# Constant matmuls and the order of all engines' work in an attention and feed-forward kernel: 70 in place of 30

## The chip, the cores and the metric

One core of a Trainium2 chip. The metric is the device time of one execution in microseconds, start to end; the figure for the kernel before is the median of 3 executions. Besides, one execution was recorded by the hardware profiler.

## What is computed

A block-sparse causal attention, and behind it a gated feed-forward layer. 4 batches, 8 heads, 768 positions, 64 values a head; 512 model columns, 1536 hidden columns; all inputs float32.

```
k_min, k_max = min, max of k over chunks of 32 positions
ub = sum_d max(q * k_min, q * k_max)          # a bound per position and chunk, causal
top_chunks = the 6 chunks with the largest ub
scores = q k^T / 8, only in those chunks and only for earlier positions
x = softmax(scores) v                          # to [3072, 512]
out = (sigmoid(x w_gate) * (x w_val)) w_out
```

## The kernel before

The 24 blocks of 128 positions are dealt out to eight units of three blocks, u0 to u7. Unit 0 takes the first block of batches 0, 1 and 2, for which no chunk has to be chosen; unit 2 takes the first block of batch 3 beside two others. A unit passes through preparing (loads, transposes, chunk minima and maxima, bounds), attention and the feed-forward layer; while TensorE does one unit's feed-forward, the next unit's attention and the preparation of the one after lie between its pieces.

Nothing of the order is decided on the chip or by a loop. The functions of the kernel only register operations with a name, the engines that may do them and what they read and write (`Plan.add`, line 48). Three long strings at the top then say everything: `ORDER` names each operation and its engine (P TensorE, A ScalarE or ACT, V VectorE or DVE, G GpSimd or POOL, S the DMA queue of SyncE), `SLOTS` gives each buffer its place, and `TIES` adds waits of one operation for another. `Plan.order` (line 77) reads them, and the kernel emits the operations in that order; every engine works its own list off from front to back, and waits where an input isn't there.

The operations that the change and the prediction speak of:

- `fl_0`, `fl_1`, ... (`keep_awake`, line 589): a constant matmul, a 128x128 block of ones times 256 columns of ones, written to a PSUM bank that nobody reads. 30 of them, all within TensorE's first 22 us.
- `kfT_b`, `qfT_b` (line 709), b = 0, 1, 2: four float32 transposes each of the first block's keys and queries; `kf16_b`, `qf16_b` (line 713) copy them out of PSUM; `scf_b` (line 748) are the scores, `expf_b_e` (line 751) the exponentials on ACT, `cmf_b_e` (line 753) the causal mask on POOL, `vc_b` (line 737) the cast of v, `pvf_b_e` (line 763), `rzf`, `xf`, `xpsf`, `xTf` (lines 766 to 779) the rest up to the transposed input of the feed-forward layer.
- `kn_u1_p`, `qn_u1_p`, `kT_u1_p`, `qT_u1_p` (`turned`, line 784), p = 0 to 3: copies and transposes of unit 1's keys and queries from the loads `k0_u1` ... `q3_u1` (line 647); `kx0`, `kx1` (line 681) their chunk minima and maxima on DVE, `kcr_u1` (line 688) the difference of these, `qf_u1_p` (line 825) and `qm_u1_p` (line 827) queries and their positive part, `kt`, `hk0`, `hk1`, `hq0`, `hq1` (lines 811 to 831) the operands of the later scores.
- `ub_u1` (line 899): 32 small matmuls for the bounds, then on DVE the choice of six chunks (`ubn`, `ubm`, `mx`, `ap`, `apt`, lines 907 to 930) and `hqm` (line 934), which carries it to the scores' operands.
- `hkp...` (line 583): eight copies of a constant pattern, 64 partitions x 1536, on any of three engines.
- `wgp`, `wg0` to `wg2`, `wv0` to `wv2`, `wo0` to `wo2` (lines 605 to 619): loads of the feed-forward weights, issued by POOL in its own list, with a cast to float16 on the way. Piece i serves the hidden blocks 4i to 4i+3, so `g_u0_8` to `g_u0_11` and `v_u0_8` to `v_u0_11` (lines 1268 and 1278: four matmuls of 384 columns each) need `wg2` and `wv2`.

All other loads are issued by SyncE, one behind the other, in the order of `ORDER`.

Of the kernel before, what the change touches and what calls it, by code (L numbers as in the profile page):

```python
# [96 lines left out]
ident=G ones16=V fl_4=P fl_2=P fl_8=P fl_3=P fl_1=P fl_0=P fl_29=P k2_u1=S kn_u1_2=A qf1_0=S kf1_0=S kf0_0=S fl_6=P fl_5=P epat0=V  # L97
ident16=V ap0=V epat=G hkp110=A hkp000=A hkp001=V kT_u1_2=P kcr0=V kt_u1_2=V hk0_u1_2=G vf1_1=G hkp011=V hkp010=G vf1_2=G hkp100=G
kf1_2=S kf0_1=S kfT_0=P kxf1=V fl_17=P fl_10=P fl_7=P kx0_u1_2=V kf16_0=V qf0_0=S qfT_0=P qf16_0=V qf1_1=S kf1_1=S kfT_1=P
kf16_1=V fl_15=P fl_16=P scf_0=P expf_0_1=A fl_19=P qf0_1=S qfT_1=P hq0=V ap1=V fl_14=P fl_9=P fl_13=P fl_11=P fl_18=P fl_12=P  # L100
qf16_1=V scf_1=P v10=G vf_0=S v16_0_0=G qf0_2=S qf1_2=S kf0_2=S expf_0_0=A cmf_0_0=G pvf_0_0=P rzf_0_0=V xf_0_0=V kx1_u1_2=V
cmf_0_1=G wgp=G kfT_2=P pvf_0_1=P qfT_2=P qf16_2=V rzf_0_1=V xf_0_1=V kxf0=V expf_1_0=A cmf_1_0=G vf_1=S vc_1=G pvf_1_0=P
rzf_1_0=V xpsf_0_0=P expf_1_1=A cmf_1_1=G pvf_1_1=P hkf0=G hk1_u1_2=A kf16_2=A scf_2=P expf_2_1=A expf_2_0=A k0_u1=S kn_u1_0=V
kT_u1_0=P xf_1_0=V fl_20=P fl_21=P wg0=G q3_u1=S qn_u1_3=A q2_u1=S rzf_1_1=V xf_1_1=V xpsf_1_1=P hq1=V xTf_1_1=V kx0_u1_0=V
kx1_u1_0=V vf_2=S wv0=G cmf_2_0=G fl_23=P xpsf_0_1=P fl_24=P fl_22=P fl_27=P xpsf_1_0=P vc_2=G xTf_1_0=V pvf_2_0=P rzf_2_0=V
xf_2_0=V q1_u1=S k3_u1=S kn_u1_3=G kT_u1_3=P hkp111=A q0_u1=S fl_28=P kx1_u1_3=V cmf_2_1=G pvf_2_1=P xpsf_2_0=P rzf_2_1=V xf_2_1=V
qT_u1_3=P qf_u1_3=V k1_u1=S qn_u1_1=A qT_u1_1=P xTf_0_0=A xTf_0_1=A qn_u1_2=A qn_u1_0=A kn_u1_1=G kT_u1_1=P kx1_u1_1=V kx0_u1_1=V
kt_u1_0=A qm_u1_3=A fl_25=P xpsf_2_1=P fl_26=P qT_u1_2=P v_0_3=S v_0_2=S v_0_1=S qf1_3=S k0_u2=S q2_u2=S k1_u2=S qf_u1_1=V
qf_u1_2=V v11=G wv1=G wg1=G hq0_u1_3=G qT_u1_0=P kt_u1_3=A hk0_u1_3=G hq1_u1_3=G wv2=G xTf_2_1=A xTf_2_0=A qf_u1_0=A qm_u1_0=A
g_u0_0=P g_u0_2=P kx0_u1_3=V kcr_f=V kcr_u1=V hkp101=V hq1_u1_0=V hkf1=V kt_u1_1=V hk0_u1_1=G wg2=G qm_u1_2=A qm_u1_1=A ub_u1=P  # L110
ubn0_u1=V ubm0_u1=V hq0_u1_1=A hq0_u1_2=A g_u0_3=P g_u0_1=P mx0_u1=V ap0_u1=V apt0_u1=V hqm0_u1_0=V v_u0_1=P v_u0_0=P v_u0_2=P
hq0_u1_0=A tanh_u0_2=A tanh_u0_1=A hg_u0_1=V ubn1_u1=V v_u0_3=P tanh_u0_3=A hg_u0_3=V ubm1_u1=V hg_u0_2=V tanh_u0_0=A hg_u0_0=V
hk0_u1_0=A hq1_u1_1=A sc_u1_0_2=P exp_u1_0_2=A sc_u1_1_2=P sc_u1_0_1=P sc_u1_0_0=P exp_u1_1_2=A sc_u1_1_0=P sc_u1_1_1=P
exp_u1_0_0=A exp_u1_0_1=A v_u0_7=P wo0=G hqm0_u1_2=G sc_u1_2_2=P exp_u1_2_2=A sc_u1_2_0=P exp_u1_2_0=A sc_u1_3_0=P sc_u1_3_2=P
exp_u1_3_2=A exp_u1_1_0=A sc_u1_3_1=P exp_u1_3_1=A exp_u1_3_0=A v16_0_3=G wo1=G v_u0_4=P sc_u1_2_1=P v_u0_6=P exp_u1_2_1=A
hk1_u1_0=G v16_0_2=G wo2=G mx1_u1=V ap1_u1=V apt1_u1=V hqm1_u1_0=V g_u0_5=P tanh_u0_5=A v_u0_5=P exp_u1_1_1=A hqm1_u1_2=A g_u0_6=P
# [285 lines left out]
def kernel(  # L402
# [192 lines left out]
    for i in range(30):  # L595
        keep_awake(i)
# [860 lines left out]
```

## Time and profile before

| | us |
|---|---|
| median of 3 executions | 281.0 (280.67 to 282.69) |
| the profiled execution | 279.88 |
| its span, first to last instruction | 278.2 |
| TensorE busy | 269.2 (97%) |
| VectorE (DVE) busy | 231.2 (83%) |
| ScalarE (ACT) busy | 180.4 (65%) |
| GpSimd (POOL) busy | 163.1 (59%) |

A row of the profile in order of time gives the start, the length, the engine, the line of the kernel, the operation, what it writes and reads, shapes, how many instructions are merged into the row, and in brackets how long the engine stood idle before and what ended that. Tile names come without their numbers: `fl<-ones` stands for all constant matmuls, `g_u` for all gate products. A row of a queue gives packets, megabytes and the share of the 16 DMA engines' time; q1 is SyncE's queue, q0 the one of POOL's weight loads. Ends of matmuls are modelled, and matmuls overlap, so that a row of several is shorter than its parts.

### The profile page before, as it was taken

The page shows a single profiled execution, that of the slowest core. Times are in us where ns is not written, and L with a number is a line of the kernel's source. Part 1 is how long each engine was busy: PE and PEld are TensorE (multiplying, and loading weights), DVE is VectorE, ACT ScalarE, POOL GpSimd, SP SyncE. Part 2 cuts the span into 40 slices and gives each one's busy share as a digit, 9 for nine tenths or more (in the row PEclk, how much of TensorE's full clock was granted, in tenths as well). Part 3 has the DMA queues.
Part 4 walks back from the last instruction along what each step waited for, and adds up shares of the span by engine and source line. Part 5 has one row for each costly group of instructions (what it writes and reads, how often), then busy time and mean ns, then how long its engine had stood idle before and what let it go on. Part 6 is the DMA issues. An engine that isn't in the chain of part 4 may idle for free.

```text
span 278.2 us, 7566 instructions
## 1 busy us (share of the span) xinstructions
PE 269.2 (97%) x2806; PEld 189.3 (68%) x2806; DVE 231.2 (83%) x686; ACT 180.4 (65%) x386; POOL 163.1 (59%) x262
## 2 busy tenths in 40 slices
PE   5979999999999999999999999999999999999995
PEld 3755658667755666557687657776888688778684
DVE  4799747687999998796999987978889998888985
ACT  6388969569858944468689979988983422341430
POOL 5797744639372873534669966724766467163440
PEclk9999999999999999999999999999999999999999
DMA  6999999999999598696896230100320033000304
GB/s 157 258 281 204 207 217 208 220 179 202 187 217 189 142 183 188 145 161 125 164 157 114 68 85 17 40 0 3 73 77 2 1 83 127 2 1 2 151 2 152
DMA packets 131717, 34.70 MB, mean 125 GB/s; under 512 B 119776, under 2 KB 128736, under 8 KB 131680
## 3 DMA queue, kind: packets, MB, share of 16 engines
q1 hardware_dynamic: 126912, 29.50, 50.6%
q0 software_dynamic: 4768, 4.72, 10.1%
q8 instruction: 22, 0.36, 0.5%
q14 instruction: 15, 0.12, 0.1%
HBM read 30.67 MB, written 6.29 MB: 133 GB/s over the span
## 4 chain that ended last, share of the span: by engine, by line
PE 87%; DMA 6%; DVE 5%; SPq 1%; issue 0%; POOL 0%; DVEq 0%
PE v_u L1259 20%; PE g_u L1259 15%; PE sc_u L957 12%; PE o_u L1308 11%; PE p_u L1082 10%; PE pv_u L990 7%; DMA wg<-in_moe_w_gate_dram 5%; PE p_g_u L1191 5%; PE ube_u L896 3%; DMA kf<-in_k_dram 1%; DVE xf L768 1%; PE kfT L709 1%; PE qfT L709 1%; PE fl L591 1%; DVE kx_u L681 1%; DVE kcr L681 1%
## 5 line engine op out<-in xcount | busy, mean ns | idle before, releaser
L968 ACT ACTIVATE att_u<-sc_u 128x512 f16<-128x512 f32 (+3 forms) x184 | 86.9, 573 | 8.6 <-PE sc_u L957 7.3
L1259 PE MATMUL v_u<-xT_u,wv 128*128 128x384 f16 x384 | 72.4, 326 | 0.0
L1280 DVE SCALAR_TENSOR_TENSOR hg_u<-gate_u,v_u 128x384 f16<-128x384 f16 x96 | 51.2, 545 | 19.3 <-ACT gate_u L1271 9.7
L1271 ACT ACTIVATE gate_u<-g_u 128x384 f16<-128x384 f32 x72 | 35.1, 499 | 40.3 <-PE g_u L1259 35.1
L1259 PE MATMUL g_u<-xT_u,wg 128*128 128x384 f16 x288 | 56.0, 326 | 0.9 <-ACT xT_u L452 0.5
L1259 PEld LDWEIGHTS <-wv 128*128 128x128 f16 x384 | 36.2, 98 | 20.3 <-issue 0.2
L974 POOL TENSOR_SCALAR_AFFINE_SELECT att_u<-att_u 128x384 f16<-128x384 f16 (+1 forms) x56 | 28.0, 509 | 37.4 <-ACT att_u L968 16.4
L1259 PEld LDWEIGHTS <-wg 128*128 128x128 f16 x288 | 26.7, 98 | 18.3 <-DMA wg<-in_moe_w_gate_dram 1.8
L1308 PE MATMUL o_u<-wo,hg_u 128*128 128x512 f16 x144 | 34.3, 379 | 0.0
L990 PE MATMUL pv_u<-v,att_u 128*128 128x65 f16 x640 | 26.3, 193 | 0.0
L990 PEld LDWEIGHTS <-att_u 128*128 128x128 f16 x640 | 24.2, 98 | 2.9 <-issue 0.6
L1228 DVE TENSOR_TENSOR f_g_u<-p_g_u,f_g_u 128x192 f32<-128x192 f32 (+1 forms) x72 | 24.9, 383 | 1.0 <-PE p_g_u L1191 0.4
L957 PE MATMUL sc_u<-hqe,hke 128*128 128x128 f16 (+2 forms) x220 | 25.1, 243 | 0.0
L957 PE MATMUL sc_u<-hqo,hko 128*128 128x128 f16 (+2 forms) x220 | 24.1, 243 | 0.0
L1308 PEld LDWEIGHTS <-hg_u 128*128 128x128 f16 x144 | 13.7, 98 | 13.4
L957 PEld LDWEIGHTS <-hke 128*128 128x128 f16 x220 | 16.5, 98 | 4.9 <-issue 0.6
L957 PEld LDWEIGHTS <-hko 128*128 128x128 f16 x220 | 16.4, 98 | 4.4
L673 POOL CAST v<-v 128x512 f16<-128x512 f32 x23 | 14.4, 627 | 5.8 <-DVE qf_u L863 1.8
L1271 ACT ACTIVATE gate_u<-f_g_u 128x384 f16<-128x384 f32 x24 | 11.9, 519 | 5.6 <-DVE hg_u L1280 2.9
L1011 DVE TENSOR_TENSOR x_u<-pv_u,rz_u 128x384 f16<-128x384 f32 (+1 forms) x28 | 14.6, 524 | 0.9 <-DMA xT_u<-x_u 0.6
L919 DVE MAX8 mx_u<-ubn_u 128x8 f32<-128x8 f32 (+16 forms) x152 | 12.7, 158 | 0.3
L1099 DVE SCALAR_TENSOR_TENSOR sw<-p_u,sw 128x256 f32<-128x256 f32 (+1 forms) x20 | 10.6, 528 | 2.4 <-PE p_u L1082 2.0
(187 smaller groups left out, 504.9 us busy)
## 6 DMA issues: line engine op xcount, KB each, us to landing
v<-in_v_dram SPq DMA_DIRECT2D x23, 256.0 KB, 4.7
k<-in_k_dram SPq DMA_DIRECT2D x12, 384.0 KB, 5.4
q<-in_q_dram SPq DMA_DIRECT2D x12, 384.0 KB, 5.9
out_dram<-osb_u SPq DMA_DIRECT2D x12, 256.0 KB, 3.3
out_dram<-sw SPq DMA_DIRECT2D x8, 256.0 KB, 2.1
wv<-in_moe_w_val_dram POOLq DMA_DIRECT2D x3, 512.0 KB, 9.8
wo<-in_moe_w_out_dram POOLq DMA_DIRECT2D x3, 512.0 KB, 17.6
qf<-in_q_dram SPq DMA_DIRECT2D x8, 128.0 KB, 3.3
```

Source lines behind the costliest of these rows:

```text
L673: plan.add(f"v16_{b}_{ib}", {POOL: pool(H * D)}, lambda e: nc.gpsimd.tensor_copy(v16[b % 2][:, ib, :, 0:D], at(t)), reads=[t], writes=[("v ...
L957: nc.tensor.matmul(at(t)[:, o:o + 128 * m], hk[b % 2][e_][:, p, 128 * jb:128 * jb + 128], hq[u.side][e_][:, p, 128 * x:128 * (x + m)], sta ...
L968: plan.add(f"exp_{u.name}_{h}_{y}", {ACT: act(n)}, lambda e, t=t, att=att, b0=b0, n=n: nc.scalar.activation(at(att)[:, b0:b0 + n], at(t), ...
L974: nc.gpsimd.affine_select(out=dv, in_=dv, compare_op=ALU.is_ge, fill=0.0, base=0, pattern=[[0, u.m], [1, 128]], channel_multiplier=-1)
L990: nc.tensor.matmul(at(pv)[:, last, x, :], at(att)[:, c:c + 128], v16[b % 2][:, jb, h, :], start=(jb == 0), stop=(jb == ib))
L1011: plan.add(f"x_{u.name}_{p}", {DVE: dve(u.t)}, lambda e: nc.vector.tensor_tensor(at(x_).rearrange("p a (e d) -> p e a d", e=2), at(pv)[:, ...
L1082: nc.tensor.matmul(at(to)[:, side], a(j)[:, i], b(j)[:, i], start=j == i == 0, stop=j == 2 and i == 1)
L1228: plan.add(f"{p}_{name}", {POOL: pool2(192 * n), DVE: dve(192 * n)} if slow else {DVE: dve(192 * n)}, lambda e: both(e).tensor_tensor(dst( ...
L1259: nc.tensor.matmul(at(t), w16[:, c, 128 * fb:128 * fb + 128], at(u.xt)[:, c, :], start=(c == 0), stop=(c == 3))
L1271: plan.add(f"tanh_{u.name}_{fb}", {ACT: act(T, not seven[0])}, lambda e, gv=gv, gate=gate: nc.scalar.activation(at(gate), gv(), AF.Tanh, s ...
L1280: plan.add(f"hg_{u.name}_{fb}", {DVE: dve(T)}, lambda e, vv=vv, gate=gate, hg=hg, fb=fb: nc.vector.scalar_tensor_tensor(at(hg)[:, fb % 2], ...
L1308: nc.tensor.matmul(at(o), at(hgs[fc // 2])[:, fc % 2, 128 * tb:128 * tb + 128], wo16[:, fc, lo:hi], start=(fc == 0), stop=(fc == NFB - 1))
```

## The change

In the code one number changes:

```
-    for i in range(30):
+    for i in range(70):
         keep_awake(i)
```

All else is in the three strings. They are written anew: the order of every engine's list but SyncE's loads, the places of the buffers, and the ties (137 before, 129 after).

The beginning of each list, up to the first products of the feed-forward layer (names alone):

```
TensorE before: 9 fl, kT_u1_2 kfT_0, 3 fl, qfT_0 kfT_1, 2 fl, scf_0, 1 fl, qfT_1, 6 fl, scf_1 pvf_0_0 kfT_2 pvf_0_1 qfT_2
  pvf_1_0 xpsf_0_0 pvf_1_1 scf_2 kT_u1_0, 2 fl, xpsf_1_1, 1 fl, xpsf_0_1, 3 fl, xpsf_1_0 pvf_2_0 kT_u1_3, 1 fl, pvf_2_1 xpsf_2_0
  qT_u1_3 qT_u1_1 kT_u1_1, 1 fl, xpsf_2_1, 1 fl, qT_u1_2 qT_u1_0 g_u0_0 g_u0_2 ub_u1
TensorE after: 29 fl, kfT_0 kT_u1_2, 1 fl, qfT_0, 9 fl, scf_0 kfT_1, 7 fl, qfT_1, 1 fl, qfT_2 pvf_0_0, 1 fl, scf_1, 1 fl, pvf_0_1, 1 fl,
  kfT_2, 2 fl, xpsf_0_0 xpsf_0_1, 5 fl, scf_2 pvf_1_0, 2 fl, pvf_1_1, 2 fl, xpsf_1_0 kT_u1_0 qT_u1_3 xpsf_1_1 pvf_2_0, 3 fl,
  pvf_2_1, 1 fl, kT_u1_3 xpsf_2_0 qT_u1_1 kT_u1_1, 1 fl, xpsf_2_1, 2 fl, qT_u1_0 qT_u1_2, 2 fl, g_u0_0 g_u0_2 ub_u1
POOL before: ident epat hk0_u1_2 vf1_1 hkp010 vf1_2 hkp100 v10 v16_0_0 cmf_0_0 cmf_0_1 wgp cmf_1_0 vc_1 cmf_1_1 hkf0 wg0 wv0
  cmf_2_0 vc_2 kn_u1_3 cmf_2_1 kn_u1_1 v11 wv1 wg1 hq0_u1_3 hk0_u1_3 hq1_u1_3 wv2 hk0_u1_1 wg2 wo0
POOL after: vf1_1 ident epat hkp110 v10 vf1_2 hkp000 v16_0_0 cmf_0_0 cmf_0_1 hk0_u1_2 wgp vc_1 cmf_1_0 cmf_1_1 hkf0 wg0 cmf_2_0 wv0
  cmf_2_1 kn_u1_1 v11 hq0_u1_1 wv1 wg1 wv2 kcr_u1 hq1_u1_3 wg2 hq0_u1_0 hqm0_u1_2 wo0
```

54 operations change their engine. Of those in the first 25 us, among others: qf16_0, qf16_1, qf16_2, qf_u1_3, kt_u1_1 and hkp011 go from DVE to ACT, kcr_u1 from DVE to POOL, xTf_0_0, xTf_0_1, xTf_2_0, hk1_u1_2 and kt_u1_0 from ACT to DVE, vc_2 and kn_u1_3 from POOL to ACT, hq0_u1_1 from ACT to POOL, and the pattern copies change places between the three.

Of TensorE's work from g_u0_0 to v_u0_8, that is up to the first product that needs `wg2`, the set of operations is the same before and after, in a slightly different order. The loads by SyncE keep their order throughout, and so do the weight loads by POOL; the stores and the transposes by DMA on SyncE's queue stand at other places between the loads from unit 0's last store on.

More of the change, by code (lines that the diff above doesn't have):

```diff
@@ L96 @@
 ORDER = """
[L97 to L116, printed above, removed]
@@ new lines @@
+v_0_3=S v_0_2=S v_0_1=S qf1_3=S k0_u2=S q2_u2=S k1_u2=S wv1=G wg1=G wv2=G xTf_2_0=V g_u0_0=P g_u0_2=P hq1_u1_0=V kx1_u1_3=V
+kcr_u1=G qm_u1_0=A ub_u1=P hq1_u1_3=G wg2=G hk0_u1_3=A hkp101=A hk0_u1_1=V g_u0_1=P tanh_u0_1=A ubn0_u1=V ubm0_u1=V mx0_u1=V
+ap0_u1=V apt0_u1=V hqm0_u1_0=V g_u0_3=P tanh_u0_3=A ubn1_u1=V ubm1_u1=V v_u0_3=P v_u0_1=P tanh_u0_2=A hkf1=A hq0_u1_3=A v_u0_2=P
+hg_u0_2=V hg_u0_3=V hg_u0_1=V hq1_u1_1=A v_u0_0=P tanh_u0_0=A hg_u0_0=V hq0_u1_0=G sc_u1_0_2=P exp_u1_0_2=A sc_u1_1_2=P
@@ L374 @@
+sw3_u67_1<c12_u7 sw2_u67_2<c22_u7
 """
```

522 lines of the change are left out of this document (271 added, 251 removed).

## The prediction

> **What bounds the kernel now.** I read the page's totals (the table above) first, then the busy time by stage, then TensorE's waits, then the chain of waits, and only then the first 28 us in order of time.
>
> ```profile
> 0.00:22.80 22.80, 17.44 (x138) 12.59 (x139) 16.74 (x43) 14.43 (x25) 18.22 (x34) 1.00 1.00 229
> 22.80:40.45 17.65, 17.25 (x157) 10.26 (x156) 12.71 (x49) 13.75 (x33) 10.16 (x19) 1.00 1.21 209
> 40.45:274.30 233.85, 233.85 (x2508) 166.16 (x2509) 200.69 (x595) 152.23 (x329) 134.72 (x211) 1.00 0.53 108
> ```
> ```profile
> PE g_u L1259 <- ACT xT_u L452: 0.5, 1, 0.5
> PE g_u L1259 <- DMA wg<-in_moe_w_gate_dram: 0.2, 1, 0.2
> ```
>
> The columns of the stages are length, busy time of PE, PEld, DVE, ACT and POOL, granted clock, DMA share, GB/s. From 40.45 us to 274.30 TensorE is busy 233.85 of 233.85 us: nothing can be won there unless its work shrinks, and it doesn't. The second fence is the whole list of TensorE's waits from 22.8 to 274 us: two. So the change can win only by moving the point at 40.45 us, where the feed-forward of unit 0 takes up the third piece of the gate weights, to an earlier time.
>
> ```profile
> 26.18 14.22 DMA wg<-in_moe_w_gate_dram
> ...
> 40.45 1.48 PE g_u L1259 x8
> ```
>
> The chain of waits passes there through the load wg2: issued at 26.18, landed at 40.40. It reads as if an earlier issue would land earlier. The queues say otherwise:
>
> ```profile
> q1 hardware_dynamic: 4999, 2.13, 97.7%
> q0 software_dynamic: 222, 0.21, 16.7%
> ```
> ```profile
> q0 software_dynamic: 2345, 2.32, 85.5%
> q1 hardware_dynamic: 2713, 0.99, 34.8%
> ```
> ```profile
> L612 POOL DMA_DIRECT2D wg<-in_moe_w_gate_dram x1: 801/801/801, 15.9 to 15.9; - x1
> DMA to landing us min/median/max: 7.3/7.3/7.3
> ...
> L613 POOL DMA_DIRECT2D wv<-in_moe_w_val_dram x1: 746/746/746, 23.4 to 23.4; - x1
> DMA to landing us min/median/max: 13.5/13.5/13.5
> ```
>
> First fence: packets, MB and share of the 16 DMA engines from 12 to 20 us; second: from 24 to 40. Both sums are over 100%: the engines are full. wg0 lands at 15.9 + 7.3 = 23.2, wv2 at 23.4 + 13.5 = 36.9, wg2 at 40.4: 3.5 us a piece at the end, one behind the other. wg2 stood behind wv2 for 10.7 of its 14.22 us. What sets 40.40 is when POOL's queue of weights begins to be served and that it never runs dry, not the issue of wg2. And TensorE reaches the same point only about 0.2 us before: loads and TensorE are level.
>
> **The change part by part.** (1) 40 more constant matmuls, 29 of the 70 in a row ahead of the first transpose kfT_0.
>
> ```profile
> 1.12 2.10 PE L591 MATMUL fl<-ones 128*128 128x256 f16 x9 [1.12 <-DVE ones L587]
> 5.81 1.09 PE L709 MATMUL kfT<-ident,kf 128*128 128x128 f32 x4 [0.90 <-DMA kf<-in_k_dram]
> ...
> 9.85 0.61 PE L746 MATMUL scf<-qf,kf 64*128 64x128 f16 x8
> 10.39 0.40 PE L591 MATMUL fl<-ones 128*128 128x256 f16 x1
> 11.43 1.01 PE L591 MATMUL fl<-ones 128*128 128x256 f16 x6
> ...
> 12.89 0.63 PE L709 MATMUL kfT<-ident,kf 128*128 128x128 f32 x4
> 17.65 0.27 PE L591 MATMUL fl<-ones 128*128 128x256 f16 x1
> 17.87 0.49 PE L591 MATMUL fl<-ones 128*128 128x256 f16 x3
> ```
>
> One constant matmul follows the next after (2.10 - 0.40) / 8 = 0.21 us early and (0.49 - 0.27) / 2 = 0.11 us late: TensorE runs at half speed until about 11.6 us, although the stages' clock column says 1.00. It worked without a pause from 5.81 on, and had pauses of 0.82 and 0.90 us before. With 29 in a row from 1.12 there is no pause. All slow, they end at 1.12 + 29 x 0.21 = 7.2; if full speed comes at 4.9 us (18 slow, 11 fast) at 6.1. kfT_0 thus begins 0.3 to 1.4 us later than at 5.81, and takes 1.09 - 0.63 = 0.46 less where full speed has come.
>
> The Trainium skill, TensorE: Matmul & The Clock Gate, Part 1, says that about 3.4 us of sustained activity release the full clock. This trace needed 5.8 us from 5.81; by the skill's figure, an estimate, the release would fall between 4.5 and 8 us, and the end of the 29 in the same span as above.
>
> What the slow stretch cost: four groups of transposes (the first at 5.81, the last before 11.43) at about 1.09 against 0.63, 4 x 0.46 = 1.8 us. The other constants cost 0 while TensorE waits (the rows of the wait lists and 17.44 busy of 22.8 show the cover); each costs 0.11 us where it stands ahead of work that is ready, such as the last two ahead of g_u0_0.
>
> (2) The weights' queue. On POOL, ahead of the first weight load wgp, hk0_u1_2 is put in and nothing taken out, but the masks of block 0 come earlier, since qf16_0 goes from DVE, where it stood behind two other pieces, to ACT.
>
> ```profile
> 4.00 1.13 SPq L636 DMA_DIRECT2D qf<-in_q_dram  x2
> 9.01 0.45 SPq L631 DMA_DIRECT2D vf<-in_v_dram  x1
> ```
> ```profile
> vf<-in_v_dram SPq DMA_DIRECT2D x3, 256.0 KB, 3.8
> qf<-in_q_dram SPq DMA_DIRECT2D x5, 128.0 KB, 3.3
> ```
> ```profile
> 9.84 0.61 POOL L673 CAST v<-vf 128x512 f16<-128x512 f32 x1
> 11.65 1.22 POOL L753 TENSOR_SCALAR_AFFINE_SELECT attf<-attf 128x512 f16<-128x512 f16 x2 [1.19 <-ACT attf L751]
> 12.82 0.79 POOL L610 DMA_DIRECT2D wg<-in_moe_w_gate_dram x1
> 13.63 0.66 POOL L753 TENSOR_SCALAR_AFFINE_SELECT attf<-attf 128x512 f16<-128x512 f16 x1
> 15.91 0.80 POOL L612 DMA_DIRECT2D wg<-in_moe_w_gate_dram x1
> ```
>
> The queries of block 0, issued at 4.00, land 3.3 us later at 7.3; transposes and copy, 0.63 each, and the nine constants that lie beside the copy let scf_0 start at 8.6 at full speed, and near its 9.85 at half. The masks start 1.8 later as before (11.65 - 9.85), though not ahead of 10.45, where the cast of v ends: 10.45 to 11.65. With 1.2 for the two and 0.5 for hk0_u1_2, wgp goes out at 12.2 to 13.3, against 12.82. From wgp to wg0 there are the same four POOL operations, 15.91 - 13.63 = 2.3 us, and its first, vc_1, waits for vf_1, landed at 9.01 + 3.8 = 12.8. Issue of wgp 0.8 included, wg0 goes out at 15.3 to 16.4: 0.6 earlier to 0.5 later. Ends for the landings: +0.5, and -1.6, if wg0 besides gets ahead of the last load of v in q1 (256 KB in pieces of 256 bytes, 1024 packets, by 4999 packets in 8 us). I take -0.6, the early end of POOL's own rows, since full speed by 7 us is likelier than not.
>
> wv1, wg1 and wv2 now stand in a row, and are issued by about 23.3 (rival B). wg0 lands at 22.6 and the next piece some 3.5 us after it, so the queue doesn't run dry. wg2 leaves about 2 us earlier, worth nothing by the above.
>
> (3) TensorE's own way to 40.2. It runs without a gap from the first work that has its weights.
>
> ```profile
> L647 SPq DMA_DIRECT2D kq_u<-in_k_dram x1: 467/467/467, 14.0 to 14.0; - x1
> ...
> DMA to landing us min/median/max: 5.4/5.4/5.4
> ```
> ```profile
> 22.20 1.01 DVE L454 COPY qf_u<-qT_u 128x384 f32<-128x384 f32 x2
> 22.65 0.50 ACT L452 COPY qf_u<-qT_u 128x384 f32<-128x384 f32 x1
> 23.19 1.19 ACT L695 ACTIVATE qm_u<-qf_u 128x320 f32<-128x320 f32 x3
> 23.27 0.93 PEld L1259 LDWEIGHTS <-wg 128*128 128x128 f16 x7 [1.12 <-DMA wg<-in_moe_w_gate_dram]
> 23.71 0.21 DVE L688 TENSOR_TENSOR kcr<-kx_u,kcr 128x48 f32<-128x48 f32 x1
> 24.51 0.45 PE L896 MATMUL ube_u<-qf_u,kcr 64*32 64x320 f32 x1
> ```
>
> The first gate product goes on when wg0 lands (23.27), the bounds ub_u1 at 24.51, just behind ACT's last qm at 24.38. In the new order the first goes with wg0, 0.6 earlier. For the second, the last transposes stand behind k1_u1 (the first of these two fences), issued at 14.0 and landed 5.4 us later, at 19.4; copy 0.5, transposes and constants 1.2: qT_u1_0 done at 21.1. On ACT there follow eight pieces up to the last qm. Three qm take 1.19, so 0.40 a piece, eight of them 3.2: ub_u1 at 24.3, 0.2 earlier than now. TensorE then comes to wg2 at 40.2 - 0.2 = 40.0, wg2 lands at 40.4 - 0.6 = 39.8. **Sum: the start at 40.45 becomes 40.05, -0.4 us.** The clock's 1.8 us are absorbed by the wait for loads.
>
> (4) From 40.45 on: the same matmuls, the same four engines, 54 of some 1970 operations on another engine. No gain is possible in a stretch without idle time. A loss is bounded by the waits of the stage before: 0.40 in 17.65 us, over 233.85 us 5.3. I take 0, as DVE at 200.69 and the others at less leave room.
>
> The profiled execution took 279.88 us (span 278.2 and 1.68 around it), 1.1 under the median of 281.0. 279.88 - 0.4 = 279.5, and against the median 281.0 - 0.4 = **280.6 us**.
>
> **The rivals.** A, the clock's 1.8 us come through whole, because the weights land that much earlier: 281.0 - 1.8 = 279.2. For it: the chain of waits from 5.81 to 25.7 runs over TensorE and DVE. Against: wg0 would have to land at 21.4, from full DMA engines. The Trainium skill, DMA: Bandwidth & Descriptors, Queues, rings and completion order, says that each DMA engine takes turns between the queues that have work; the trace agrees from 24 to 40 us (2345 and 2713 packets) and not from 12 to 20 (222 and 4999), and where it holds an earlier issue of wg2 gains nothing.
>
> B, slower: the difference kcr_u1, on DVE before, now stands on POOL behind hq0_u1_1 and three weight issues, and ub_u1 waits for it. It decides as soon as qf_u1_1 is ready after 24.3 - 0.25 - 3 x 0.8 - 0.5 = 21.1 (an issue at 0.79 to 0.80 by POOL's rows above, kcr_u1 at DVE's 0.21 and a little more, a copy 0.5). DVE had it ready at about 22.7, halfway through the row at 22.20; I expect 20.6, since its transpose now stands ahead of the ones that wait for k1_u1. As late as before, ub_u1 would begin at 22.7 + 3.2 = 25.9, 1.4 late, and TensorE with it: 281.0 + 1.4 = 282.4.
>
> C, the order behind 40.45 us leaves TensorE waiting at half the rate of the stage before: 280.6 + 2.7 = 283.3. For it: POOL takes over work of DVE and ACT; against: the idle time of the three engines.
>
> **How the numbers follow.** My forecast 0.52 (279.5 to 281.4), A 0.13, B 0.18, C 0.17. The likeliest is 280.6. The range from 278.8 to 283.3 takes in A and B and half of C. One per cent, 2.8 us, is about what tells a change from none here: faster than that 0.05 (A with a quick later order), slower 0.08 (the worse half of C), the rest 0.87. My own case alone spans 279.5 (landings 1.6 earlier, the bounds in step) to 281.4 (0.5 later).
>
> **What would show it.** Right: constant matmuls 0.11 us apart from some time between 4.9 and 7.2 us; transposes at 0.63 from the first; wg0 issued near 15.3 and landed near 22.6; wg2 issued near 24 and still landing between 39.3 and 40.4; TensorE without waits behind it. Wrong: wg2 landing by 38.5 (A); ub_u1 released by POOL after 24.6 (B); waits of TensorE after 45 us that sum to over 1 us (C).

## The result and the profile after

The changed kernel takes 283.16 us (median of 7, 282.6 to 285.01), the kernel before 281.0 (median of 7, 280.21 to 282.69): a ratio of 1.0087, 95% interval 1.0062 to 1.0111. Here and below, medians and ratios are of the executions within 1.5% of a kernel's fastest; a few took longer, up to 290.0 us. The forecast was 280.6. The time lies inside the range, but the sign is wrong: 2.4 us are lost by the ratio (281.0 x 0.0087), 2.2 by the medians, where 0.4 were to be won. The profiled executions stand 3.2 us apart (span 281.4 against 278.2); that is more than the medians show, because the one of before was 1.1 us under its median.

TensorE's start after the change, from the timeline (start, length, engine, line; lines are 5 higher than before):

```profile
1.12 5.32 PE L596 MATMUL fl<-ones 128*128 128x256 f16 x29 [1.12 <-DVE ones L592]
6.28 0.60 PE L714 MATMUL kfT<-ident,kf 128*128 128x128 f32 x4
...
7.67 1.15 PE L596 MATMUL fl<-ones 128*128 128x256 f16 x9
9.72 0.40 PE L751 MATMUL scf<-qf,kf 64*128 64x128 f16 x8 [0.90 <-DVE kf L459]
```

The clock does what was forecast: 29 constants take 5.32 us, so the later of them stand 0.11 apart, and the first transposes take 0.60 instead of 1.09. Yet scf_0 starts at 9.72, 0.13 earlier than before and not 1.2. It waits 0.90 us for kf16_0, a copy on VectorE. VectorE's queue, and then GpSimd's, in the same microseconds:

```profile
4.00 2.29 DVE L459 COPY hke<-epat 64x1536 f16<-64x1536 f16 x2 [2.15 <-POOL epat L571]
...
6.99 1.47 DVE L602 CAST ident<-ident 128x128 f16<-128x128 f32 x1
8.39 0.67 DVE L724 TENSOR_REDUCE kx_f<-kfT 128x16 f32<-128x512 f32 x1
8.99 0.67 DVE L459 CAST kf<-kfT 128x512 f16<-128x512 f32 x1
```
```profile
4.04 1.84 POOL L461 COPY hko<-epat 64x1536 f16<-64x1536 f16 x1
...
6.65 1.73 POOL L461 COPY hke<-epat 64x1536 f16<-64x1536 f16 x1
```

The first of these copies and the conversion before:

```profile
1.78 0.15 DVE L597 CAST ident<-ident 128x128 f16<-128x128 f32 x1
...
4.00 0.55 DVE L454 COPY hke<-epat 64x1536 f16<-64x1536 f16 x1 [1.66 <-POOL epat L566]
```

Two pattern copies of VectorE take 2.29 us together (one alone took 0.55 before), and the conversion ident16 1.47 us (0.15 before). The second copy and the conversion end just behind a GpSimd copy that runs beside them, which ends at 5.88 and 8.38. This use of the clock's gain was not foreseen; whether it matters, experiment h6 tells.

The weight loads on GpSimd's queue after, and the same stretch before:

```profile
15.53 0.80 POOL L617 DMA_DIRECT2D wg<-in_moe_w_gate_dram  x1
...
17.14 0.78 POOL L618 DMA_DIRECT2D wv<-in_moe_w_val_dram  x1
...
21.60 0.49 POOL L461 CAST hqe<-qf_u 64x384 f16<-64x384 f32 x1 [1.04 <-DVE qf_u L459]
22.04 0.77 POOL L618 DMA_DIRECT2D wv<-in_moe_w_val_dram  x1
22.81 0.75 POOL L617 DMA_DIRECT2D wg<-in_moe_w_gate_dram  x1
```
```profile
20.39 0.76 POOL L613 DMA_DIRECT2D wv<-in_moe_w_val_dram  x1
21.15 0.75 POOL L612 DMA_DIRECT2D wg<-in_moe_w_gate_dram  x1
21.89 0.52 POOL L456 CAST hqe<-qf_u 64x384 f16<-64x384 f32 x1
```
```profile
L617 POOL DMA_DIRECT2D wg<-in_moe_w_gate_dram x3: 750/793/801, 15.5 to 26.0; - x3
...
DMA to landing us min/median/max: 7.5/11.3/15.5
```

wg0 is issued at 15.53 and lands 7.5 us later at 23.0, as forecast within 0.4. wg2 is issued at 26.00 and lands 15.5 us later, at 41.5, not at 39.8. Between them stands a new thing: hq0_u1_1, which ran on ScalarE before, is now ahead of wv1 on the queue, waits until 21.60 for qf_u1_1, and wv1 goes out at 22.04 instead of 20.39 (the row at 21.89 before is another copy, hq0_u1_3). The packets of the two DMA queues from 24.5 to 27 us, first before, then after (packets, MB, share of the 16 engines; q0 holds the weights, q1 SyncE's loads):

```profile
q0 software_dynamic: 356, 0.35, 83.4%
q1 hardware_dynamic: 629, 0.16, 38.6%
```
```profile
q0 software_dynamic: 275, 0.27, 63.9%
q1 hardware_dynamic: 1202, 0.30, 60.1%
```

81 packets of weights fewer. At the 146 a microsecond of the stretch from 24 to 40 us (2345 in 16) that is 0.55 us of a delay at wg2; by half microseconds the weights' queue brings 48, 45 and 45 packets from 25 to 26.5 us where it brings 75 to 80 in a full one. It runs short, though never empty (before, a single half microsecond has 48).

The whole list of TensorE's waits from 22.5 us to the end after the change, and the stages up to its start at wg2 and from there on (columns as in the prediction's first fence):

```profile
PE g_u L1264 <- DVE xT_u L459: 0.9, 1, 0.9
PE g_u L1264 <- DMA wg<-in_moe_w_gate_dram: 0.5, 1, 0.5
PE sc_u L962 <- DVE sw L1104: 0.4, 1, 0.4
```
```profile
22.80:41.53 18.73, 17.28 (x158) 10.48 (x157) 11.99 (x46) 16.68 (x37) 11.94 (x23) 1.00 1.21 213
41.53:277.90 236.37, 235.59 (x2512) 166.43 (x2512) 200.45 (x594) 147.49 (x323) 138.55 (x217) 1.00 0.52 106
```

TensorE takes up wg2's product at 41.53 instead of 40.45, and needs 1.9 us more from there to its last matmul (277.93 - 41.53 = 236.4, against 274.91 - 40.45 = 234.5). The list of waits names only 0.4 of these 1.9. The rest is in stops of a few tenths that show when each operation's distance to the next is compared with that of before: at 68.6 (0.29), 154 (0.20), 204 (0.59, of which the list has 0.4), 212 (0.30) and 249 us (0.24), 1.6 together. What ends them stands on the weight loads (PEld) or on another engine's queue:

```profile
68.74 0.27 PEld L995 LDWEIGHTS <-att_u 128*128 128x128 f16 x7 [0.24 <-POOL att_u L979]
```
```profile
203.48 0.36 DVE L1176 TENSOR_TENSOR hke<-xT_u,hke 128x384 f16<-128x384 f16 x1 [1.11 <-DMA xT_u<-x_u]
203.76 0.42 DVE L1104 SCALAR_TENSOR_TENSOR sw<-p_u,sw 128x256 f32<-128x256 f32 x1
```
```profile
204.23 0.38 PE L962 MATMUL sc_u<-hqe,hke 128*128 128x384 f16 x2 [0.42 <-DVE sw L1104]
```
```profile
212.22 0.36 PEld L1196 LDWEIGHTS <-ss_g 128*128 128x128 f16 x5 [0.36 <-DVE f_g_u L1233]
```

At 68 us a mask on GpSimd is late because two copies stand ahead of it. At 204 us VectorE's queue stands for 1.11 us at tt1_u5, which waits for a transpose by DMA, and u4_u4, which TensorE needs, is queued right behind it. These two stand in the same order in the kernel before, where no such stop shows.

### The profile page after: what moved, and what is told of

The parts are those of the page before. It is cut to its first block, busy times and chain, and to the rows that moved or that the text cites. A ratio compares the mean times of both kernels' runs of the same rounds, so it can differ in the third digit from the quotient of the medians.

```text
span 281.4 us, 7639 instructions
## 1 busy us (share of the span) xinstructions
PE 272.1 (97%) x2846; PEld 191.7 (68%) x2846; DVE 231.4 (82%) x682; ACT 178.7 (63%) x384; POOL 167.6 (60%) x268
## 3 DMA queue, kind: packets, MB, share of 16 engines
HBM read 30.67 MB, written 6.29 MB: 131 GB/s over the span
## 4 chain that ended last, share of the span: by engine, by line
PE 81%; DVE 7%; DMA 6%; POOL 3%; issue 2%; DVEq 0%; POOLq 0%
PE v_u L1264 19%; PE g_u L1264 15%; PE sc_u L962 12%; PE o_u L1313 11%; PE p_u L1087 8%; PE pv_u L995 7%; DMA wg<-in_moe_w_gate_dram 6%; PE p_g_u L1196 4%; PE ube_u L901 3%; DVE f_g_u L1233 1%; DVE sw L1104 1%; DVE ox L1104 1%; DVE hke L459 1%; PE fl L596 1%; POOL epat L571 1%
## 5 line engine op out<-in xcount | busy, mean ns | idle before, releaser
L995 PE MATMUL pv_u<-v,att_u 128*128 128x65 f16 x640 | 27.3, 193 | 0.1
L995 PEld LDWEIGHTS <-att_u 128*128 128x128 f16 x640 | 24.8, 98 | 3.9 <-issue 0.6
L1233 DVE TENSOR_TENSOR f_g_u<-p_g_u,f_g_u 128x192 f32<-128x192 f32 (+1 forms) x72 | 25.5, 384 | 0.9
L962 PEld LDWEIGHTS <-hke 128*128 128x128 f16 x220 | 16.5, 98 | 5.8 <-issue 1.4
L461 POOL CAST hqo<-qf_u 64x768 f16<-64x768 f32 (+2 forms) x14 | 10.0, 712 | 6.6 <-DVE qf_u L868 4.5
L596 PE MATMUL fl<-ones 128*128 128x256 f16 x70 | 12.5, 313 | 1.3 <-DVE ones L592 1.1
```

Source lines behind the costliest of these rows:

```text
L596: plan.add(f"fl_{i}", pe(109), lambda e: nc.tensor.matmul(at(t), ones16, ones16.unsqueeze(1).to_broadcast([128, 2, 128]), start=True, stop ...
L962: nc.tensor.matmul(at(t)[:, o:o + 128 * m], hk[b % 2][e_][:, p, 128 * jb:128 * jb + 128], hq[u.side][e_][:, p, 128 * x:128 * (x + m)], sta ...
L995: nc.tensor.matmul(at(pv)[:, last, x, :], at(att)[:, c:c + 128], v16[b % 2][:, jb, h, :], start=(jb == 0), stop=(jb == ib))
L1233: plan.add(f"{p}_{name}", {POOL: pool2(192 * n), DVE: dve(192 * n)} if slow else {DVE: dve(192 * n)}, lambda e: both(e).tensor_tensor(dst( ...
```

## The experiments

All times are medians; ratios are to the kernel before on the same chip, with 95% intervals. Its medians were 280.65 to 281.04. The ratios are not the quotients of the medians and differ from them by up to 0.2% (0.6 us), so a difference of a few tenths of a microsecond is read from the traces and not from the times.

**Start against rest.** At v_u0_7, where TensorE stands at 31 us, both orders have done the same set of operations. So they can be joined there: the buffers' places behind the joint are renamed to fit.

```diff
 h1: ORDER = after[.. v_u0_7] + before[v_u0_7 ..]     70 constants
 h2: ORDER = before[.. v_u0_7] + after[v_u0_7 ..]     30 constants
```

> The changed order up to v_u0_7 (TensorE at 31 us), the order of before from there; 70 constants. Theory S (start and rest each lose on their own): the start brings wg2 1.1 us later and TensorE's block g_u0_10 starts at 41.5, the old rest adds no wait, so 1.1 us over the kernel before, a ratio of 1.004 (1.003 to 1.006). Rival W (the later waits are echoes of the late start: work that comes 1 us late to the later stages): the old rest stalls too, ratio 1.008 or more. Rival R (only the rest loses, the late wg2 is made up later): ratio within 1.002 of 1.

> The order of before up to v_u0_7, with its 30 constants, and the changed order from there. Theory S: wg2 lands at about 40.4 as before, the stops of TensorE behind 42 us (at 68.6, 154, 204, 212 and 249 us in the changed kernel) are all there, about 1.9 us together, ratio 1.007 (1.005 to 1.009). Rival W: they go with the late start, ratio within 1.002 of 1. Rival R: as the changed kernel, 1.008 or more.

h1: 281.68 us, 1.0021 (0.9995 to 1.0047). h2: 282.24 us, 1.0064 (1.0043 to 1.0084). 0.0021 + 0.0064 is 0.0085, nearly all of the 0.0087. By the ratios the rest loses 1.8 us and the start 0.6, less than S put on it. By the medians, and in the traces, the rest loses 1.4 (from wg2's product to the end of the last matmul h2 needs 235.83 us, the kernel before 234.47). In h2's trace, with the start of before, the stops at 68, 154 and 211 us are there again (0.29, 0.32, 0.30), in h1 none of these three: they belong to the later order and are no echoes of a late start. The other two are not so clear. In place of the one at 249, h2 has 0.11 at 251. The one at 204, the longest of the five, is missing in h2, and in h1, with the old rest, one of 0.38 stands at 203 us: it does not belong to the later order. So three stops, 0.9 us, are what the trace shows of the later order's loss.

W falls. R is not excluded by the times, as both its ratios touch the intervals; against it speaks h1's trace, where wg2 lands as late as in the changed kernel (41.8 and 41.5) and nothing of that is made up later (234.84 us from its product to the end, 234.47 before). h2's trace also says how far this point moves by itself: with the start of before TensorE comes to wg2's product at 41.23 there, at 40.45 in the kernel before.

**The constants by themselves.**

```diff
 h3, TensorE before: 9 fl
+   5 fl
    kT_u1_2
+   12 fl
    kfT_0          (all 17 in one bank of PSUM)
 h5: the same, the 17 in rotating banks
 h10: as h5, and POOL: cmf_0_1 -wgp cmf_1_0 +wgp vc_1
 h4, TensorE after: 9 fl instead of 29 ahead of kfT_0
```

> The kernel before with 17 more constants ahead of kfT_0 and nothing else (5 ahead of kT_u1_2, 12 behind it). The clock is full from about 5 us and the transposes take 0.63 instead of 1.09. Theory of the prediction: scf_0 comes up to 1.2 us earlier than 9.85, the loads absorb it, wg2 lands within 0.3 us of 40.4, ratio within 0.002 of 1. Rival A (the 1.8 us of slow clock come through): ratio 0.994. Rival K (the constants themselves cost: they hold TensorE past kf0_0): ratio 1.002 or more.

285.07 us, 1.0161 (1.0141 to 1.0181). By its number and by its cause this is rival K: the constants hold TensorE long past 5.81, when the kernel before starts kfT_0. But the timelines of h3 (recorded in an execution of 290.0 us) and, below, of h5 show that h3 tests something else than the changed kernel's constants:

```profile
5.42 3.85 PE L604 MATMUL fl<-ones 128*128 128x256 f16 x12
```
```profile
4.47 1.47 PE L604 MATMUL fl<-ones 128*128 128x256 f16 x12
```

In one bank the constants stand (3.85 - 0.27) / 11 = 0.33 us apart, in rotating ones (1.47 - 0.27) / 11 = 0.11, both at the full clock: kfT_0 right behind them takes 0.62 and 0.66. One constant takes 0.27 us in both. In h3 each begins 0.06 us behind the end of the one before, as if it waited for it; in h5 they overlap. In h3 kfT_0 came at 9.11, 3.3 us late, and the time is 4 us longer.

> As h3, but the 17 constants go to rotating banks of PSUM, not all to one (where they stood 0.33 us apart at the full clock). Theory of the prediction: constants 0.21 and then 0.11 us apart, kfT_0 at 6.0 to 6.5 and 0.63 long, scf_0 0.5 to 1.2 us ahead of 9.85, wg2 between 40.4 and 41.2 as in the two kernels with the start of before, ratio within 0.003 of 1. Rival A: the clock's 1.8 us come through, ratio 0.994. Rival K (more constants cost whatever their bank): ratio 1.003 or more.

282.81 us, 1.0055 (1.0022 to 1.0088), single executions from 279.92 to 284.0. By the number this is rival K's; A falls. kfT_0 starts at 5.89 and scf_0 at 9.58, so the clock brings 0.27 us there, less than the theory of the prediction had. In the profiled execution, one of 284.0 us, wg2 lands at 40.31, and this stands in the list of TensorE's waits:

```profile
PE pv_u L1003 <- POOL att_u L987: 2.3, 1, 2.3
```

The loads of v, in SyncE's queue, now land late: v_0_1 at 38.79 against 30.07, and GpSimd's cast of it holds back the mask that the product waits for. A possible cause is that with the earlier start the weights take turns ahead of v; h10 asks that. There is a second loss: TensorE pauses for 0.89 and 1.29 us between 17.6 and 20.1 us, behind copies of loads that landed late, and the granted clock is 0.50 from 21.3 to 24.7 us. So even the bare constants don't bring the forecast -0.4 in this order.

> As h5 (before with 17 more constants, ratio 1.0055, between 279.9 and 284.0 us from one execution to the next), with the load wgp issued behind cmf_1_0 on GpSimd's queue, at about 13.2 instead of 12.35 us. Theory Q (a weight load that is issued while vf_2 and q1_u1 still wait in SP's queue slows them, and the v loads behind them): vf_2 lands by 16 and q1_u1 by 17 us (h5: 17.75 and 18.79), v_0_2 by 22.5 (32.25), the stop of 2.3 us for att_u2 goes, ratio within 0.002 of 1. Rival K (the constants and the work they bring forward cost by themselves): ratio 1.004 or more again.

281.62 us, 1.0040 (1.0011 to 1.0069), single executions from 280.18 to 284.04. The number is K's lower bound, Q's values lie in the interval: inconclusive. wgp went out at 12.92, not 13.2. In the profiled execution, a longer one of 285.98 us, vf_2 and q1_u1 land early (16.56 and 17.05), as Q said, but v_0_2 and v_0_1 late all the same (32.86 and 39.44), and the stop for att_u2 is 4.7 us long instead of gone. That the weights take turns ahead of v because they are issued early is not shown. What decides in which execution v comes late stays open.

> The changed kernel with 20 of the 29 constants at its start taken away (50 left). Theory P (the gain of the clock is lost to copies that DVE and GpSimd run against each other until 8.4 us, so that the early clock is worth little): scf_0 moves by under 0.5 us and the time stays within 0.002 of the changed kernel's, ratio to before 1.007 to 1.011. Rival A (the clock is worth something that the later losses hide): scf_0 comes 1 us or more later than 9.72 and the ratio is 1.012 or more. Rival K (the constants are what costs): ratio 1.005 or less.

283.57 us, 1.0117 (1.0092 to 1.0141), against 1.0087 for the changed kernel: the 20 constants win at most a little (the intervals meet). K falls: in the changed order the constants are not what costs. Between P and A it stays open, as scf_0 moved from 9.72 to 10.52, by 0.8, between the two theories' bounds.

**The copies that hold each other up.**

```diff
 h6 = h1 with
 DVE:  epat0 +ident16 hkp001 hkp100 kcr0 hkp010 -ident16 kxf1
 POOL: epat +v10 +vf1_2 hkp110 -v10 -vf1_2 hkp000        tie: hkp110 behind DVE's hkp010
```

> As h1 (the changed start, the old rest), with GpSimd's two pattern copies hkp110 and hkp000 behind VectorE's three, a tie between them, ident16 right behind epat0, v10 and vf1_2 ahead. Theory P (DVE and GpSimd hold each other up, and the transposes' gain goes there): hkp100 takes 0.55 instead of 1.81 and ident16 0.16 instead of 1.47, kf16_0 ends by 8.4, scf_0 starts at 8.5 to 8.8 instead of 9.72; the loads then absorb it and the time is that of h1 (ratio 1.002) within 0.003. Rival A: the 1 us comes through, ratio 0.998 or less. Rival Q (the copies take as long whoever runs beside them): scf_0 stays within 0.3 us of 9.7.

281.62 us, 1.0023 (1.0001 to 1.0044). VectorE's two copies and kf16_0, and TensorE's scf_0:

```profile
4.00 1.25 DVE L469 COPY hke<-epat 64x1536 f16<-64x1536 f16 x2 [2.06 <-POOL epat L581]
...
7.39 0.68 DVE L469 CAST kf<-kfT 128x512 f16<-128x512 f32 x1
```
```profile
8.73 0.40 PE L761 MATMUL scf<-qf,kf 64*128 64x128 f16 x8
```

scf_0 is 1 us earlier, at 8.73, the time the same as h1's. GpSimd's two copies take 1.46 us each here, against 1.84 and 1.73. The hold-up is real, and no part of the loss: the microsecond goes into the wait for loads, as theory P had it. Q and A fall.

**What brings wg2 late.**

```diff
 h9  = h1 with  POOL: hkf0 -wg0 cmf_2_0 +wg0 wv0
 h11 = h1 with  POOL: v11 -hq0_u1_1 wv1 wg1 wv2 +hq0_u1_1
 h12 = h1 with  DVE:  (behind xf_2_1) +xTf_2_0 qf_u1_1 ... qf_u1_2 -xTf_2_0 hq1_u1_0
 h14 = h1 with both, and ACT: +qm_u1_0 hq0_u1_2 -qm_u1_0
 h16 = the changed kernel with h11's move
 h17 = the kernel before with  POOL: v11 -wv1 -wg1 hq0_u1_3 hk0_u1_3 +wv1 +wg1 hq1_u1_3 wv2
```

> As h1, with the load of wg0 issued behind cmf_2_0 on GpSimd's queue, at about 17.2 instead of 15.5 us. Theory Q1 (wg0 ahead of v_0_2 costs the weights the time in which they have the DMA engines alone): v_0_2 lands by 22 us instead of 26.6, the later weights come sooner and wg2 lands at 40.4 to 41.0 instead of 41.8; ratio 1.000. Rival Q2 (the weights' queue ends later by what its start is later): wg0 lands at 24 us or later, wg2 at 42 to 43, ratio 1.004 or more.

281.68 us, 1.0017 (0.9991 to 1.0043). v_0_2 lands at 21.31, as Q1 wants, but in h1 it had landed at 22.0 already (26.6 is the changed kernel's), so that little was to be won there. wg2 lands at 42.48, the latest but two of all, and not by 41.0. By that Q1, my own first theory, falls: the place of wg0 before or behind a load of v isn't it. Of Q2, wg2's landing came, wg0's (23.2, not 24) and the time didn't.

> As h1 (changed start, old rest), with hq0_u1_1 behind wv2 on GpSimd's queue, so that wv1, wg1 and wv2 are issued from 20.6 instead of 22.0 us. Theory of the prediction (the issue time of the later weights is worth nothing, their queue is full then): wg2 lands at 41.5 to 42 as in h1, ratio 1.002 (0.000 to 1.004). Rival I (the later issue is what brings wg2 late): wg2 at 40.4 to 41.0 and the ratio 0.999 or less.

280.95 us, 1.0014 (0.9989 to 1.0038). The times of h1 and h11 can't be told apart by their intervals; the traces can: wv1 goes out at 20.32, wg2 lands at 40.37 instead of 41.81, and TensorE takes it up at 40.94 instead of 41.86, now without a wait: its own work gets there no earlier. By the landing rival I holds, by the ratio the prediction's theory.

> As h1, with xTf_2_0 on VectorE right behind its transposes (at about 20.5 instead of 23.5 us), so that the first block g_u0_0 no longer waits for it. Theory D (the arrival of wg2 sets the time, TensorE being late before it costs nothing): g_u0_0 at 23.2 to 23.4 instead of 23.9, the wait at wg2 grows by as much, ratio 1.002 as h1. Rival T (TensorE's own lateness is the cost): ratio 0.999 to 1.000.

281.62 us, 1.0032 (1.0012 to 1.0052). g_u0_0 starts at 23.15 instead of 23.92, and TensorE takes up wg2's product at 41.94, as late as h1: D holds. Where wg2 is late, TensorE's own way there costs nothing.

> As h11 (changed start with hq0_u1_1 behind the weights, old rest; median 280.95, wg2 at 40.37, TensorE there at 40.94), with xTf_2_0 early on VectorE as in h12 and, on ScalarE, qm_u1_0 ahead of hq0_u1_2. Theory E (once wg2 comes in time, TensorE's own lateness is the bound): g_u0_0 at 23.2, g_u0_10 at 40.4 to 40.6, ratio 0.998 to 1.000. Rival D (the arrival of wg2 is the bound all the same): ratio 1.001, as h11.

281.12 us, 1.0023 (0.9990 to 1.0057). g_u0_0 at 23.14, wg2 at 40.33, but TensorE at it only at 40.94: two new stops (0.41 in ub_u1 for the last qm, 0.45 at sc_u1_0_1) took what was gained. Neither theory holds, and by its ratio no version beats the kernel before.

> The changed kernel with hq0_u1_1 behind wv2 on GpSimd's queue and nothing else. Theory N (the weights' queue ran dry): the software queue's packets stay above 60 in every half microsecond from 23 to 27 us (45 to 48 in three of them in the changed kernel), wg2 lands at 40.3 to 40.8 instead of 41.5, ratio 1.006. Rival M (the order of the v loads sets it): wg2 at 41.2 or later, ratio 1.008 or more.

282.24 us, 1.0054 (1.0031 to 1.0077). The packets from 24.5 to 27 us, the landing of the gate weights, and TensorE's start at wg2's product:

```profile
q0 software_dynamic: 389, 0.38, 90.5%
q1 hardware_dynamic: 392, 0.10, 30.4%
```
```profile
L626 POOL DMA_DIRECT2D wg<-in_moe_w_gate_dram x3: 747/791/798, 15.5 to 25.7; - x3
...
DMA to landing us min/median/max: 7.6/13.2/15.3
```
```profile
41.03 1.15 PE L1273 MATMUL g_u<-xT_u,wg 128*128 128x384 f16 x6
```

389 packets instead of 275, wg2 lands 15.3 us after 25.67, at 41.0 (forecast 40.3 to 40.8; M's 41.2 or later didn't come either). TensorE's row shows no wait any more, but the weight load of this product waits 0.41 us for wg2, and the product begins 0.36 us behind the matmul before it, where 0.16 is the distance without a wait: 0.2 are left. One move of one instruction regains 0.9 us (1.0087 to 1.0054, intervals overlapping).

> The kernel before with wv1 and wg1 behind hq0_u1_3 and hk0_u1_3 on GpSimd's queue, so that wv1 is issued at about 22.3 instead of 20.4 us. Theory N: the software queue drops to under 50 packets a half microsecond for 1.5 us at 24 to 26 us, wg2 lands 0.7 to 1.5 us later than 40.4, TensorE waits for it, ratio 1.003. Theory of the prediction (the issue time is worth nothing): wg2 within 0.3 us of 40.4 to 41.2, ratio within 0.001 of 1.

281.93 us, 1.0029 (1.0006 to 1.0052): the same fault made in the kernel before.

```profile
q1 hardware_dynamic: 1510, 0.44, 77.0%
q0 software_dynamic: 201, 0.19, 45.5%
```
```profile
PE v_u L1269 <- DMA wv<-in_moe_w_val_dram: 0.8, 2, 0.5
PE g_u L1269 <- DMA wg<-in_moe_w_gate_dram: 0.7, 2, 0.5
```

wv1 at 22.86, 201 packets instead of 356, wg2 lands at 42.79, and TensorE waits for weights. wg2 comes 2.4 us later than before, more than N's 0.7 to 1.5; the time is N's. In its direction theory N holds both ways. Over the profiled executions: with wv1 issued by 20.5 us wg2 landed at 40.33 to 41.18 (before, h2, h11, h13 to h16), with wv1 at 21.9 or later at 41.48 to 42.79 (the changed kernel, h1, h4, h6, h7, h9, h12, h17). h5, with wv1 at 21.24, is apart: 40.31, with the loads of v late. h10 (20.34 and 39.8) and h3 (23.04 and 42.3), recorded in long executions, lie on the same sides.

**The stops behind 42 us.**

```diff
 h7 = the changed kernel with
 POOL: hqm1_u2_2 -hq1_u2_3 cm_u2_5 cm_u2_1 +hq1_u2_3
 POOL: -hqm1_u5_2 cm_u5_3 cm_u5_4 +hqm1_u5_2 cm_u5_2
 DVE:  tt0_u5 +u4_u4 tt1_u5 -u4_u4
 h13 = h2 with these three;  h15 = h7 with h16's move
```

> The changed kernel with three moves behind 42 us: hq1_u2_3 behind cm_u2_1 on GpSimd, hqm1_u5_2 behind cm_u5_4 on GpSimd, u4_u4 ahead of tt1_u5 on VectorE. Theory S (the later order makes stops of its own, each behind one instruction that stands ahead in a queue): the stops at 68.6, 154 and 204 us (0.29, 0.2 and 0.59) go, the one at 212 (0.30) stays, ratio 1.009 less 0.004, so 1.005. Rival W (they are echoes, and another wait takes each place): ratio unchanged at 1.007 to 1.011.

282.85 us, 1.0063 (1.0037 to 1.0090), on the side of S, with W's values from 1.007 in the interval: inconclusive. In its profiled execution a load of the start came late, so that the place of wg2 isn't read here. Behind it, stops of 0.18 at 157, 0.15 at 206 and 0.30 at 213 us are left.

> As h2 (the start of before, the changed rest, ratio 1.0064), with the three moves of h7 behind 42 us. Theory S (the stops of the changed order are its own and local): the stops at 68, 153 us go, and with them 0.6 to 0.7 us, ratio 1.004; a stop at 211 stays. Rival W (another wait takes each place): ratio 1.006 or more.

281.51 us, 1.0029 (1.0014 to 1.0045) against h2's 1.0064: 1.0 us comes back by the ratios (the two intervals just meet), 0.7, as expected, by the medians and in the traces (235.11 us from wg2's product to the end, 235.83 in h2). The weight loads of the matmuls at 68 us, first in h2, then here:

```profile
68.42 0.27 PEld L999 LDWEIGHTS <-att_u 128*128 128x128 f16 x7 [0.24 <-POOL att_u L983]
```
```profile
68.63 0.45 PEld L999 LDWEIGHTS <-att_u 128*128 128x128 f16 x10
```

No wait is left there. At 154 one of 0.18 stands in place of 0.32, right behind the end of the copy that was moved (hqm1_u5_2), an exchange as W has it; the one at 210 us (0.30) stays, as expected. On the whole S holds.

> The changed kernel with hq0_u1_1 behind wv2 and the three moves of h7. If the dry queue (0.7 us) and the stops that the three moves take away (1.0 us) are the loss: 2.4 less 1.7, ratio 1.002 to 1.004. If something else in the change costs as much: 1.006 or more.

281.54 us, 1.0025 (1.0002 to 1.0048), as expected. Four instructions moved, three on GpSimd's queue and one on VectorE's, bring 1.7 of the 2.4 us back (the interval of the changed kernel begins at 1.0062), with all 70 constants, the early clock and the other moves in place. Of what is left, the trace shows stops of 0.30 at 210 and 0.18 at 155 us, and TensorE's start at wg2's product at 40.83 against 40.45. What the move on VectorE (u4_u4) adds is not shown: the stop at 204 that it was meant for is missing without it in h2 and h4 too.

## Why the prediction was wrong

(1) **The constants.** The clock was full at about 5 us and kfT_0 started at 6.28, inside the forecast's 6.1 to 7.2. From the first constant at 1.12 that is about 4 us (in h5, where kT_u1_2 at 4.08 already takes 0.56 instead of 0.88, 3 us). The Trainium skill's 3.4 us of sustained activity (TensorE: Matmul & The Clock Gate, Part 1) lies between the two. That the 1.8 us of clock would be absorbed by loads was right: in h6 scf_0 comes a microsecond earlier and the time stays. Of the 1.2 us by which scf_0 was to come earlier only 0.13 arrived, as the copies of VectorE and GpSimd that hold each other up were not in the sum; h6 puts the price of that at nothing. Rival A is out.

(2) **The weights' queue: here the first step failed.** wgp and wg0 were issued and wg0 landed within 0.4 us of the forecast (hk0_u1_2 stood ahead of wgp before too; new is only that it stands right ahead of it). wv2 went out at 23.54, as forecast; wg2 at 26.00, not near 24, behind kcr_u1, which waited for VectorE until 25.14. The sentence that failed is "so the queue doesn't run dry", with the issue of the later loads priced at nothing: wg2 landed at 41.5 instead of 39.8, and the late issue of wv1 cost 0.9 us (h16, intervals overlapping) and 0.8 us (h17). I had compared the landing of wg0 (22.6) with the issue of wv1, and taken the interval between landings, 3.5 us, as the time a queue holds. But the queue thins out before the last load in it has landed: q0 is short from 24.5 to 26.5 us, and wv0 lands at 26.37. And an issue takes time to come to packets: the first of all on q0 came at 14.5 us, 2.1 after wgp's issue began (before: at 15.4, 2.6 after; wg0's, issued at 15.91, from about 19). From wv1's 22.04 that gives 24.1 to 24.6, where the shortage begins; why full flow is back only at 26.5 the trace doesn't show. In the meantime q1 takes the turns: 1202 packets instead of 629. The same lag touches a reading of the prediction: from 12 to 20 us, where it counted 222 packets against 4999, the weights' queue sent none before 15.4 and 9 between 17 and 19. Whether it had any to send in these gaps the trace doesn't show, so that row is no test of whether queues take turns.

(B) The rival B had the right cause and the wrong victim. qf_u1_1 was ready at 21.53, behind B's limit of 21.1, and hq0_u1_1 stood waiting on GpSimd for it. The price was asked of kcr_u1 and ub_u1; kcr_u1 waited for VectorE instead, and ub_u1 came at 25.32, not 25.9. What the wait cost went through the loads queued behind it. I had the three weight issues in the sum only as something that kcr_u1 stands behind.

(3) **TensorE's way to wg2.** -0.4 forecast; h1 gives +0.6 (-0.1 to 1.3). TensorE was 1.0 late at ub_u1 (25.32 against 24.3), as the first product waits 0.9 us for xTf_2_0, now the last in a row of VectorE's copies. That move from ScalarE to VectorE was in the diff and not in my sum. It cost nothing in the end (h12), since wg2 came later still. But the term was wrong by itself: where the weights come in time, TensorE reaches wg2's product at 40.94 (h11), not at the 40.0 of the sum.

(4) **The rest: here the second step failed, and the larger one.** 0 taken, 1.8 us measured by h2's ratio (1.4 by the medians), inside the bound of 5.3 and near rival C's 2.7. C's time, 283.3, is the measured 283.16, with too much for the rest and too little for the start. The argument was that the engines have idle time enough. They have: VectorE is busy for 200.45 of 236.37 us. But the stops don't come from an engine that is full. The ones at 68 and 154 us come from one instruction that stands ahead of a needed one in GpSimd's queue, in an order written by hand: h13 takes the first away and shortens the second, and VectorE and GpSimd are as busy as in h2 (200.94 and 138.39 us of 235.7, against 200.75 and 138.01). What makes the one at 212 (0.30) was not tried, and about 0.3 us of the rest's loss in h2's trace stands in no stop that was named.

## What to carry to other kernels

Where a load sets the time, look for the first instruction ahead of any issue in that queue that can wait, and ask whether the queue still has packets to send when the issue comes, not whether the load before has landed. A stage without idle time has no gain to give but a loss to take: a new order can cost in each place where a needed piece is queued behind one that waits, whatever the engines' shares of busy time. A list of waits leaves out what is short: the sum of distances between operations, against the same operations before, found 1.6 us where the list had 0.4.

## What the runs showed of the hardware

VectorE's fp16 copies, and its conversion ident16, and GpSimd's copies hold each other up. hkp100 ended at 6.29, 0.41 us behind GpSimd's hkp110, and ident16 (0.15 us alone) at 8.46, 0.08 behind hkp000. The Trainium skill says that the port pair they share is locked for a whole instruction and that the later one fully blocks (SBUF — State Buffer, SBUF: two separate sides); the trace agrees. GpSimd's two copies took 1.84 and 1.73 us, and 1.46 where h6 keeps them apart. VectorE's other work beside GpSimd was not stretched: before, the reduction kxf1 and the conversion kf16_0 out of PSUM took 0.69 and 0.68 beside copies of GpSimd.

Constant matmuls that all write one bank of PSUM stand 0.33 us apart, three times the 0.11 of rotating banks, at the full clock (h3 and h5). Whether the bank costs that, or a wait of each for the end of the one before, these runs don't separate; each begins 0.06 us behind that end.

A mean clock near 1 can hide a stretch at half. In h5's recorded execution the mean is 0.994, and the granted clock is 0.50 from 21.3 to 24.7 us, after two pauses of TensorE of 0.89 and 1.29 us; three transposes take 0.85 us there instead of 0.55. In h13's it is 0.50 from 16.5 to 19.8 us, without harm to the time (280.88).

Executions of h5 differ by 4 us (279.92 to 284.0), where those of h9 lie within 1.3 (281.13 to 282.4); in h5's recorded one, of 284.0, the loads of v were late. What makes them late is open.
